# First ten attention units in another order, nine routing constants on GpSimd, second routing tables thirteen steps later

## The chip, the core and the metric

The kernel runs on one core of one Trainium2 chip. The metric is the device time of one execution in microseconds (us). A core has five engines that run their own instruction streams in order: TensorE (PE, matmuls and transposes through the array), VectorE (DVE), ScalarE (ACT), GpSimd (POOL) and SyncE (SP, which here issues most DMAs). An instruction waits at the head of its stream until the semaphores that it names have been raised; what stands behind it waits too.

## The reference

The program is an attention followed by a mixture of experts, with one expert for each token:

```python
q_n, k_n = rmsnorm(q, g_q), rmsnorm(k, g_k)      # 8 batches, 12 heads, 448 tokens, 64 wide
scores = scale * np.matmul(q_n, k_n.transpose(0, 1, 3, 2))
scores = scores - np.max(scores, axis=-1, keepdims=True)
attn = np.exp(scores)
attn = attn / (np.sum(attn, axis=-1, keepdims=True) + 1e-09)
x = np.matmul(attn, v)                           # as 3584 tokens x 768
...
logits = x @ w_gate + modality_bias[modality_id]
e_idx = np.argmax(logits, axis=1)                # one of 8 experts
...
h = np.maximum(x[mask] @ w1[e], 0.0)             # 768 -> 1024
out[mask] = gate_w[mask, None] * (h @ w2[e])     # 1024 -> 768
```

## The kernel before

The attention is cut into 48 units, one for each pair of heads of a batch, and each unit into seven slots; step n = 7u + j is slot j of unit u. The program runs a loop over n from -22 on, and two tables of numbers written out in the source decide at which n each piece of work is issued (PLAN) and, for the second part, at which of its steps (MOE). Since every engine runs its stream in order, these tables are the schedule.

For a unit, q and k are loaded (`ld`, SP's queue), squared and summed (`sq`), turned into reciprocal roots (`rs`), scaled (`norm`, tile xrw), transposed on PE (`tr`, L807: tk for k, tq for q) and copied out of PSUM as a high part and a rounded remainder (tile xw; `parts`, `va`, `vs` choose engine and step). ACT rounds them into w1w, and DMAs on SP's queue move them (the rows w1w<-xw and w2ha<-xw). `sa` is a matmul of the high parts; DVE reduces it to row maxima (at_hlw<-sa). `mt` (L905) transposes the seven maxima, ACT copies them (xw<-mt) and a DMA puts them beside q as an extra row, so that `st` (L921) gives scores less their maximum. ACT exponentiates st from PSUM (r2w<-st, at_w2lw<-st), GpSimd and DVE add up the sums, and `av` (L965) multiplies with v. Lists in PLAN say for which q or k the sum of squares is made on GpSimd (`ps`, a tree of six additions), on ACT (`pa`, eight activations that each accumulate a row) or on DVE; `nv` lists scalings on DVE; `warm` counts matmuls on constants (L1149) that are put between the others on PE.

The seven `sa` of a unit stand ahead of its own `st` slots: `first` gives the step of the first one and `sastep` the distance to the next. In the kernel before, the `mt` of unit 2 is issued at step 5 and its last `sa` at step 6.

Routing constants are made by `tables_consts`, 25 small DVE instructions from index tiles that GpSimd writes at the start. The program puts them on a list (`slow`) at the end of unit 0, and a few are taken from it at every slot.

The second part runs in slots of 256 tokens of one expert, 24 steps each: 8 steps of mm1 (`ph`, L555, x times w1) and 16 of mm2 (`py`, L586). w1 comes as f32 (r) and is split into a rounded part (ACT, CAST w1w<-r) and a remainder (DVE, w1w<-r,w1w), one pair for each quarter of two of the six row blocks; w2 likewise (w2lw<-r2w). `xtr` and `xcp` transpose the tokens and split them (xrw, xw). After mm1, ACT writes the relu hhw and DVE its remainder hlw from PSUM. Which tokens and experts the later slots take is computed by `tables2`, some 60 small DVE instructions (tb_..., L56). From the step under the key 'tab2' on they are on a list from which `little` pops a fixed number at each step; `flush` is the step at which what is left is issued at once. `get` starts the reading of a slot's lists and `fin` finishes them.

Of the kernel before, what the change touches and what calls it, by code (L numbers as in the profile page):

```python
# [1602 lines left out]
```

## Time and profile before

| | |
|---|---|
| median of three runs | 1047.12 us (1045.88 to 1047.6) |
| the profiled execution | 1046.28 us, of which the span is 1044.6 us |
| PE busy | 1002.7 us, 96% of the span, mean granted clock 0.987 |
| DVE, ACT, POOL busy | 768.8 us (74%), 696.9 us (67%), 706.9 us (68%) |
| PE busy, 0 to 110 us | 94.71 us at a clock of 0.92 |
| PE busy, 110 to 500 us | 381.53 us at 1.00 |
| PE busy, 500 to 700 us | 190.62 us at 0.98 |
| PE busy, 700 us to the end | 335.84 us at 0.99 |

The span runs from the first to the last instruction of the program, and the execution's own time is 1.68 us longer. Busy time is the sum over an engine's instructions without overlaps. The clock is that granted to PE, as a share of 2.4 GHz; 0.50 is 1.2 GHz. PE's idle time and its time at half clock are the two ways in which the span exceeds PE's work.

### The profile page before, as it was taken

The page shows a single profiled execution, that of the slowest core. Times are in us where ns is not written, and L with a number is a line of the kernel's source. Part 1 is how long each engine was busy: PE and PEld are TensorE (multiplying, and loading weights), DVE is VectorE, ACT ScalarE, POOL GpSimd, SP SyncE. Part 2 cuts the span into 40 slices and gives each one's busy share as a digit, 9 for nine tenths or more (in the row PEclk, how much of TensorE's full clock was granted, in tenths as well). Part 3 has the DMA queues.
Part 4 walks back from the last instruction along what each step waited for, and adds up shares of the span by engine and source line. Part 5 has one row for each costly group of instructions (what it writes and reads, how often), then busy time and mean ns, then how long its engine had stood idle before and what let it go on. Part 6 is the DMA issues. An engine that isn't in the chain of part 4 may idle for free.

```text
span 1044.6 us, 19480 instructions
## 1 busy us (share of the span) xinstructions
PE 1002.7 (96%) x6299; PEld 797.9 (76%) x6299; DVE 768.8 (74%) x1499; ACT 696.9 (67%) x1409; POOL 706.9 (68%) x733
## 2 busy tenths in 40 slices
PE   8889999999999999999899899999999999999996
PEld 7656665665666565555449899999999999999996
DVE  6788887888888788887678966676775667666740
ACT  5768998988999898887564554545554555455630
POOL 4677878888888889888866646556554665566221
PEclk8989999999999999999999899999999999999999
DMA  7767787767787777755753111122181221121070
GB/s 184 167 176 195 190 195 181 185 162 199 171 194 181 184 186 165 189 133 130 193 175 81 43 35 54 48 55 63 39 278 51 63 49 35 43 61 55 26 258 34
DMA packets 174741, 133.32 MB, mean 128 GB/s; under 512 B 119084, under 2 KB 168336, under 8 KB 173476
## 3 DMA queue, kind: packets, MB, share of 16 engines
q1 hardware_dynamic: 148900, 90.63, 36.4%
q0 software_dynamic: 23856, 41.28, 12.5%
q8 instruction: 52, 0.85, 0.4%
q14 instruction: 61, 0.50, 0.1%
q10 hardware_dynamic: 1872, 0.06, 0.1%
HBM read 139.06 MB, written 24.18 MB: 156 GB/s over the span
## 4 chain that ended last, share of the span: by engine, by line
PE 80%; DVE 7%; issue 4%; DMA 3%; ACT 3%; POOL 1%; ACTq 0%; SPq 0%; POOLq 0%; DVEq 0%
PE ph L555 21%; PE py L586 18%; PE st L921 15%; PE av L965 12%; PE sa L894 5%; PE tr L807 3%; DMA w1w<-xw 2%; PE pm L980 2%; DVE at_hlw L55 2%; DVE xw L55 1%; DVE xrw L55 1%; ACT w1w L55 1%; DVE w1w L55 1%; PE pm L996 1%; PE sa L885 1%
## 5 line engine op out<-in xcount | busy, mean ns | idle before, releaser
L555 PE MATMUL ph<-xw,w1w 128*128 128x256 f32 x2016 | 248.5, 285 | 6.0 <-DVE w1w L55 3.8
L55 DVE TENSOR_REDUCE at_hlw<-sa 128x1 f32<-128x448 f32 x336 | 204.4, 613 | 66.9 <-PE sa L894 52.8
L555 PEld LDWEIGHTS ph<-xw,w1w 128*128 128x128 f32 x2016 | 246.2, 193 | 7.9 <-DVE w1w L55 4.2
L921 PE MATMUL st<-w1w 128*128 128x448 f32 x480 | 175.0, 413 | 6.8 <-ACT at_w2lw L55 5.8
L921 PEld LDWEIGHTS st<-w1w 128*128 128x128 f32 x480 | 83.6, 190 | 98.3 <-ACT xw L55 24.2
L55 POOL DMA_INDIRECT xrw<-x_d,i x112 | 133.6, 1193 | 36.1 <-issue 31.9
L55 DVE TENSOR_TENSOR w1w<-r,w1w 128x512 fp32r<-128x512 f32 (+1 forms) x180 | 108.7, 648 | 32.1 <-ACT w1w L55 32.1
L55 POOL DMA_INDIRECT r2w<-in_moe_w_dram,tb_w2i x48 | 53.3, 1110 | 116.2 <-DVE w2lw L55 110.6
L55 ACT ACTIVATE hhw<-ph 128x512 fp32r<-128x512 f32 x56 | 33.5, 599 | 128.1 <-PE ph L555 128.1
L55 ACT ACTIVATE at_w2lw<-st 128x448 f32<-128x448 f32 x168 | 89.8, 540 | 39.5 <-PE st L921 37.2
L586 PE MATMUL py<-w2lw,hhw 128*128 128x384 f32 x448 | 115.0, 334 | 0.0
L894 PE MATMUL sa<-w1w 128*128 128x448 f32 x282 | 107.4, 382 | 7.5 <-DVE at_hlw L55 6.5
L55 ACT CAST w1w<-xw 64x448 fp32r<-64x448 f32 x188 | 105.6, 561 | 9.8 <-DVE xw L55 6.0
L921 PE MATMUL st<-w1w,w2ha 65*128 65x448 f32 x288 | 101.1, 371 | 2.1 <-DMA w1w<-xw 2.1
L55 ACT CAST w1w<-r 128x512 fp32r<-128x512 f32 (+1 forms) x180 | 102.0, 637 | 0.0
L55 DVE TENSOR_TENSOR w2lw<-r2w,w2ha 128x1536 fp32r<-128x1536 f32 x28 | 49.2, 1758 | 71.2 <-ACT w2ha L55 67.8
L55 ACT ACTIVATE r2w<-st 128x448 f32<-128x448 f32 x168 | 90.0, 540 | 15.2 <-PE st L921 9.5
L55 POOL TENSOR_TENSOR r2w<-r2w 128x448 f32<-128x448 f32 (+1 forms) x69 | 79.2, 1150 | 23.5 <-DVE r2w L55 10.8
L55 POOL TENSOR_TENSOR xrw<-r,at_hlw 112x512 f32<-112x512 f32 x89 | 93.5, 1052 | 1.9 <-POOL w1w L55 0.9
L55 ACT ACTIVATE yw<-py,lt 128x384 f32<-128x384 f32 x55 | 29.0, 577 | 81.3 <-issue 66.6
L586 PEld LDWEIGHTS py<-w2lw,hhw 128*128 128x128 f32 x448 | 81.0, 188 | 0.0
L55 POOL TENSOR_TENSOR r2w<-r2w,at_w2lw 64x448 f32<-64x448 f32 (+1 forms) x46 | 53.1, 1158 | 33.3 <-DVE r2w L55 19.9
(316 smaller groups left out, 2134.3 us busy)
## 6 DMA issues: line engine op xcount, KB each, us to landing
w1w<-xw SPq DMA_DIRECT2D x312, 112.0 KB
r<-in_q_dram SPq DMA_DIRECT2D x48, 224.0 KB
r<-in_k_dram SPq DMA_DIRECT2D x48, 224.0 KB
w2ha<-xw SPq DMA_DIRECT2D x72, 112.0 KB
x_d<-at_w2hb SPq DMA_DIRECT2D x8, 672.0 KB
x_d<-yw SPq DMA_DIRECT2D x8, 672.0 KB
r2w<-in_v_dram SPq DMA_DIRECT2D x24, 128.0 KB
at_w2lw<-in_v_dram SPq DMA_DIRECT2D x24, 128.0 KB
```

Of the source, the lines that this page charges most:

```text
L55: return fn(*a, **kw)
L555: PE.matmul(ps[:, i], lhsT=lt_, rhs=rt_[:, c], start=n == 0, stop=n == 17)
L586: PE.matmul(ps[n][:, :384], lhsT=lt_[:, j, 128 * t : 128 * t + 128], rhs=rt_[:, 384 * n : 384 * n + 384], start=j == 0 and m == 0, stop=j ...
L807: PE.transpose(sp[:, c], src[:, c], idn[:CP, :CP])
L885: PE.matmul(ps[:, :S], lhsT=qm_b[u % 2], rhs=hi_b[u % 2][1], start=True, stop=True)
L894: PE.matmul(ps[:, :S], lhsT=t["qq"][:, h, a : a + 128], rhs=t["kk"][h], start=True, stop=True)
L921: PE.matmul(ps[:, :S], lhsT=l, rhs=t["qq"][:, h] if first else t["ql"][:, h], start=first and (j != 3 or h == 0), stop=not first and (j != ...
L965: PE.matmul(t["av"][o : o + 64, :S], lhsT=vv[r, u_ % 3, j], rhs=t["p"][r, j], start=c == (0, 3)[u_ % 2], stop=c == (3, 2)[u_ % 2])
L980: PE.matmul(R[g][32 * i : 32 * i + 32, :S], lhsT=sel[m], rhs=T[u + i // 2]["cs"][:, i % 2 ^ i // 2], start=m == 0, stop=False, tile_positi ...
L996: PE.matmul(sm[32 * i : 32 * i + 32, :S], lhsT=wg[:, (4 * g + i) % NP], rhs=T[4 * g + i]["xt"], start=False, stop=True, tile_position=(0, ...
```

## The change

Three things change. PLAN has other numbers for the first ten units (steps, engines of single operations, constant matmuls) and for the hand-over to the second part; the `mt` of unit 2 now stands behind all seven of its `sa`. The first nine instructions of `tables_consts` are on GpSimd and are issued behind the first load; the other 16, now `lanes_consts`, stay on DVE and go on the list at the end of unit 5. In MOE, `tables2` begins at step 20 in place of 7 (slot 0's second layer is steps 8 to 23), with 4 instructions for a step in place of 3, and the steps of slots 1 to 5 are written out.

```diff
-PLAN = {'g2': 8, ... 'rushat': 32, ...
...
-('tk', 0): -19, ('tq', 0): -18, ('sa', 0): -15, ... ('mt', 0): -5, ... ('mt', 2): 5, ... ('sa', 2): 0,
-'sastep': {3: 1, 4: 1, 1: 0.5, 2: 1, 0: 1},
-'ps': [(3, 0), (8, 1), (9, 1), (6, 1)], 'pa': [(5, 1), (5, 0), (9, 0), (7, 0)],
...
+PLAN = {'g2': 6, ... 'rushat': 33, ...
...
+('tk', 0): -17, ('tq', 0): -18, ('sa', 0): -14, ... ('mt', 0): -6, ... ('mt', 2): 10, ... ('sa', 2): 2,
+'sastep': {3: 1, 4: 0.7, 1: 0.5, 2: 0.5, 0: 0.7, 6: 1, 5: 1},
+'ps': [(0, 0), (2, 0), (3, 0), (4, 1), (5, 1), (6, 1), (7, 1)],
+'pa': [(2, 0), (3, 1), (4, 1), (5, 1), (6, 1), (7, 0), (9, 0), (9, 1)],
...
-MOE = {'little': 3, ... 'tab2': 7, 'flush': 37, ... ('fin', 3): 42,
+MOE = {'little': 4, ... 'tab2': 20, 'flush': 38, ... ('fin', 3): 37, ... ('xtr', 3, 1): 66, ('xcp', 3, 1): 68,
...
     def tables_consts():
         for tf, ti in iotas:
-            V.tensor_copy(out=tf, in_=ti)
+            GP.tensor_copy(out=tf, in_=ti)
         for w in (0, LW // 2):
-            V.tensor_copy(out=ltb[:, :, :, w].bitcast(I32), in_=i_tok)
-        V.tensor_scalar(out=ie8, in0=i_e[:, 0:NE], scalar1=float(NE), scalar2=None, op0=ALU.add)
+            GP.tensor_copy(out=ltb[:, :, :, w].bitcast(I32), in_=i_tok)
+        GP.tensor_scalar(out=ie8, in0=i_e[:, 0:NE], scalar1=float(NE), scalar2=None, op0=ALU.add)
         for t in (i_ebase, zb[0][:, NCH]):
-            V.tensor_scalar(out=t, in0=i_e[:, 0:NE], scalar1=float(NT), scalar2=None, op0=ALU.mult)
+            GP.tensor_scalar(out=t, in0=i_e[:, 0:NE], scalar1=float(NT), scalar2=None, op0=ALU.mult)
+
+    def lanes_consts():
         V.tensor_scalar(out=pq, in0=ip, scalar1=5, scalar2=None, op0=ALU.arith_shift_right)
...
         load(0)
+        tables_consts()
         load_gains()
...
             if i == 0:
-                slow += deferred(tables_consts) + deferred(gate_consts)
+                slow += deferred(gate_consts)
+            if i == 5:
+                slow += deferred(lanes_consts)
```

At the start of the program, GpSimd's stream had, between the index tiles (IOTA) and the first step of unit 0's reciprocal roots (at_hlw), nothing. Now it reads:

```order
L55 IOTA i_tok 112x32
L55 CAST i_e<-i_e_i 128x16
L55 CAST i_s<-i_s_i 128x18
L55 CAST i_p<-i_p_i 128x1
L55 CAST i_w_105<-i_w_i 128x4
L55 COPY ltb<-i_tok 112x32 x2
L55 TENSOR_SCALAR ie_116<-i_e 128x8
L55 TENSOR_SCALAR i_ebase<-i_e 128x8
L55 TENSOR_SCALAR zb_119<-i_e 128x8
L55 TENSOR_TENSOR xrw<-xrw 112x8x32
```

The nine constants have moved in ahead of the first tree of additions, which sums the squares of unit 0's q and was on DVE as one reduction.

While unit 1's scores run, DVE's stream in the kernel before holds the maxima of unit 3 (sa_3) with the constants between them:

```order
L55 TENSOR_REDUCE at_hlw<-sa_1_636 128x1
L56 CAST i_p<-i_p_i 128x1
L56 CAST i_w_105<-i_w_i 128x4
L56 COPY ltb<-i_tok 112x32
L55 TENSOR_REDUCE at_hlw<-sa_2_655 128x1
L56 COPY ltb<-i_tok 112x32
L55 SCALAR_TENSOR_TENSOR xw<-tr_1_600,gs,xw 128x448
L56 TENSOR_SCALAR ie_116<-i_e 128x8
L56 TENSOR_SCALAR i_ebase<-i_e 128x8
L56 TENSOR_SCALAR zb_119<-i_e 128x8
L55 TENSOR_REDUCE at_hlw<-sa_3_675 128x1
```

In the changed kernel the maxima of unit 3 (the third of them first) stand there with the remainders of k and q, and none of the constants is left:

```order
L55 SCALAR_TENSOR_TENSOR xw<-tr_1_626,gs,xw 128x448
L55 TENSOR_REDUCE at_hlw<-sa_3_699 128x1
L55 STREAM_TRANSPOSE at_w2hb<-at_hhw 128x14x32
L55 TENSOR_REDUCE at_hlw<-sa_4_712 128x1
L55 TENSOR_TENSOR xw<-tr_0_714,xw 128x448
L55 TENSOR_REDUCE at_hlw<-sa_5_734 128x1
```

At the beginning of slot 1 of the second part, DVE's stream in the kernel before holds the last remainders of w1 (w1w<-r1_2) with the second tables between them:

```order
L55 TENSOR_TENSOR w1w_157<-r1_2_155,w1w_157 128x2x256
L56 TENSOR_REDUCE tb_lm_6727<-tb_le_6726 128x1
L56 TENSOR_SCALAR tb_ep_6725<-tb_ep_6725,tb_lm_6727 128x18
L56 TENSOR_TENSOR tb_oh_6728<-tb_ep_6725,i_e_96 128x288
L55 TENSOR_TENSOR w1w_157<-r1_2_155,w1w_157 128x2x256
L56 TENSOR_TENSOR tb_t3_6723<-tb_dd_6722,tb_oh_6728 128x288
L56 TENSOR_REDUCE tb_js_6729<-tb_t3_6723 128x18
L56 TENSOR_TENSOR tb_t3_6723<-tb_cnt_6720,tb_oh_6728 128x288
L55 TENSOR_TENSOR w1w_157<-r1_2_155,w1w_157 128x2x256
```

In the changed kernel these remainders follow each other, and the tables begin behind them and run on to the first remainder of the relu (hlw<-ph1_0):

```order
L55 TENSOR_TENSOR w1w_157<-r1_2_155,w1w_157 128x2x256 x4
L56 TENSOR_TENSOR run7_6917<-zb0_119,i_ebase_117 128x8
...
L55 TENSOR_TENSOR w2lw_6658<-r2w_159,w2ha_160 128x1536
L56 TENSOR_REDUCE tb_ci_6923<-nbp16_122 128x16
...
L56 TENSOR_REDUCE tb_lm_6929<-tb_le_6928 128x1
L55 TENSOR_TENSOR w2lw_6658<-r2w_159,w2ha_160 128x1536
L55 SCALAR_TENSOR_TENSOR hlw_6524<-ph1_0_6987,hhw_6523 128x512
```

## Rows read from the trace of the kernel before

**Rows 1.** Busy time by engine (instructions), clock, DMA share and GB/s, in two stretches
```profile
0.00:110.00 110.00, 94.71 (x502) 66.10 (x503) 86.95 (x186) 79.61 (x225) 73.66 (x119) 0.92 0.73 182
...
120.00:130.00 10.00, 9.57 (x55) 6.20 (x48) 7.73 (x14) 9.69 (x24) 7.48 (x11) 1.00 0.80 188
```

**Rows 2.** Timeline of PE in the first units
```profile
28.97 0.28 PE L905 MATMUL mt<-idn,at_hlw 128*7 128x128 f32 x1 [0.45 <-DVE at_hlw L55]
...
37.52 0.45 PE L921 MATMUL st<-w1w 128*128 128x448 f32 x1
...
45.95 0.64 PE L921 MATMUL st<-w1w 128*128 128x448 f32 x2
...
58.31 0.74 PE L894 MATMUL sa<-w1w 128*128 128x448 f32 x1 [2.65 <-DVE at_hlw L55]
...
63.92 0.57 PE L921 MATMUL st<-w1w 128*128 128x448 f32 x1
...
83.75 0.45 PE L921 MATMUL st<-w1w 128*128 128x448 f32 x1
```

**Rows 3.** Timeline of DVE in the first units
```profile
26.05 0.62 DVE L55 TENSOR_TENSOR xw<-tr,xw 128x448 fp32r<-128x448 f32 x1 [3.00 <-DMA w1w<-xw]
...
51.20 0.18 DVE L56 COPY ltb<-i_tok 112x32 int32<-112x32 int32 x1
...
53.08 3.33 DVE L56 COPY ltb<-i_tok 112x32 int32<-112x32 int32 x1
...
79.58 1.10 DVE L56 SCALAR_TENSOR_TENSOR i_w<-p,i_p 128x1 f32<-128x1 f32 x1
```

**Rows 4.** Timeline of GpSimd in the first units
```profile
6.76 0.24 POOL L56 TENSOR_SCALAR at_hlw<-at_hlw 112x16 f32<-112x16 f32 x1 [4.62 <-DVE at_hlw L55]
...
53.01 2.25 POOL L55 TENSOR_TENSOR at_hhw<-r2w 128x448 f32<-128x448 f32 x2
55.22 1.13 POOL L55 TENSOR_TENSOR r2w<-at_w2lw 128x448 f32<-128x448 f32 x1
56.43 1.12 POOL L55 TENSOR_TENSOR r2w<-r2w,at_w2lw 64x448 f32<-64x448 f32 x1
```

**Rows 5.** Busy time by engine and clock in two stretches behind waits
```profile
60.00:65.00 5.00, 4.26 (x15) 3.75 (x16) 4.10 (x8) 3.91 (x11) 2.90 (x7) 0.53 0.94 246
585.00:590.00 5.00, 5.00 (x23) 5.00 (x24) 4.73 (x22) 0.54 (x2) 4.08 (x4) 0.50 0.27 84
```

**Rows 6.** ACT's groups by form, 0 to 110 us: sums of squares by row
```profile
L55 ACT ACTIVATE xrw<-r 112x64 f32<-112x64 f32 x32 | 7.7, 242 | 0.0
```

**Rows 7.** Timeline of PE, slots 1 to 3 of the second part
```profile
578.79 1.83 PE L555 MATMUL ph<-xw,w1w 128*128 128x256 f32 x14
...
585.00 17.85 PE L555 MATMUL ph<-xw,w1w 128*128 128x256 f32 x127 [2.78 <-DVE w1w L55]
602.69 0.52 PE L586 MATMUL py<-w2ha,hhw 128*128 128x384 f32 x2
...
619.33 17.43 PE L555 MATMUL ph<-xw,w1w 128*128 128x256 f32 x144
...
656.35 0.38 PE L555 MATMUL ph<-xw,w1w 128*128 128x256 f32 x1 [1.51 <-ACT xw L55]
657.07 5.18 PE L555 MATMUL ph<-xw,w1w 128*128 128x256 f32 x41 [0.34 <-DVE xw L55]
```

**Rows 8.** Timeline of DVE, slot 1 of the second part
```profile
572.92 0.69 DVE L55 TENSOR_TENSOR w1w<-r,w1w 128x512 fp32r<-128x512 f32 x1
...
584.26 0.69 DVE L55 TENSOR_TENSOR w1w<-r,w1w 128x512 fp32r<-128x512 f32 x1
...
588.11 1.75 DVE L55 TENSOR_TENSOR w2lw<-r2w,w2ha 128x1536 fp32r<-128x1536 f32 x1
...
590.33 0.68 DVE L55 SCALAR_TENSOR_TENSOR hlw<-ph,hhw 128x512 fp32r<-128x512 f32 x1
...
607.23 3.70 DVE L55 TENSOR_TENSOR w1w<-r,w1w 128x512 fp32r<-128x512 f32 x6
```

More of the change, by code (lines that the diff above doesn't have):

```diff
@@ L34 @@
 ET = mybir.EngineType
-PLAN = {'g2': 8, 's1n': 11, 's1r': 1.1, 'mA': (), 'lA': (), 'pj': (2, 3, 6, 5, 2, 3, 4), 'rtj': 5, 'rushat': 32, 'pe': 't', 'ave': (8, 8, 8, 8), 'avo': (15, 15, 15), 'av3': 9, 'ord': (3, 0, 1, 5, 4, 2, 6), 'xt': (10, 17), 'sm': 4, 'la': 4, 'rc': 6, 'csv': (1,), 'csj': (4, 5), 'csd': (1, 0), 'cse': (2, 2), 'sa': 14, 'mt': 6, 'tk': 22, 'tq': 19, 'nq': 29, 'nk': 25, 'sk': 49, 'sq': 50, 'rs': 46, 'ld': 58, 'first': {('sq', 0): -22, ('sk', 0): -22, ('nk', 0): -20, ('nq', 0): -20, ('sq', 1): -21, ('sk', 1): -20, ('sq', 2): -20, ('sk', 2): -18, ('nk', 1): -16, ('nq', 1): -14, ('tk', 0): -19, ('tq', 0): -18, ('sa', 0): -15, ('tk', 1): -15, ('tq', 1): -13, ('sa', 1): -3, ('mt', 0): -5, ('tk', 2): -7, ('tq', 2): -4, ('nq', 2): -8, ('nk', 2): -13, ('nq', 3): -6, ('nk', 3): -5, ('sq', 3): -11, ('sk', 3): -8, ('sq', 4): -10, ('sk', 4): -11, ('sq', 6): -5, ('sk', 6): 3, ('sk', 7): -6, ('sq', 8): 6, ('sk', 8): 5, ('nk', 7): 22, ('nq', 9): 37, ('tq', 3): 0, ('mt', 1): 1, ('nq', 5): 12, ('mt', 8): 48, ('rs', 0): -21, ('rs', 2): -17, ('nq', 8): 35, ('rs', 5): -6, ('mt', 2): 5, ('nq', 7): 19, ('mt', 5): 29, ('sk', 9): 14, ('tk', 9): 41, ('mt', 6): 35, ('nq', 6): 14, ('sa', 5): 20, ('rs', 8): 10, ('mt', 4): 20, ('nk', 4): 1, ('ld', 9): 5, ('tk', 5): 13, ('tk', 3): -1, ('tk', 4): 6, ('tq', 4): 10, ('ld', 1): -22, ('ld', 2): -21, ('ld', 3): -17, ('ld', 4): -19, ('ld', 5): -21, ('tk', 8): 33, ('sa', 3): 7, ('mt', 3): 18, ('tq', 8): 38, ('nk', 9): 38, ('ld', 6): -18, ('nk', 5): 3, ('sa', 2): 0, ('sq', 5): -15, ('tk', 7): 27, ('tq', 7): 31, ('nq', 4): -3, ('sa', 7): 35, ('tk', 6): 20, ('sq', 9): 19, ('nk', 6): 17, ('sa', 6): 28, ('tq', 9): 45, ('nk', 8): 28, ('sk', 5): -12, ('tq', 5): 15, ('ld', 8): -1, ('sq', 7): -2, ('rs', 1): -19, ('ld', 7): -11, ('tq', 6): 23}, 'rs0': {0: 0, 1: 1, 2: 2, 5: 0, 8: 0}, 'sastep': {3: 1, 4: 1, 1: 0.5, 2: 1, 0: 1}, 'start': -22, 'warm': {5: 5, -6: 14, -18: 1, -17: 4, -19: 1, 4: 1, 3: 1, -5: 1, -22: 10, -11: 3, -4: 0, -20: 1}, 'warmn': 1, 'early': 1, 'late0': 1, 'pmp0': 2, 'ramp': 10, 'pmp': (0, 0, 1, 0, 0, 1, 0), 'nv': [(5, 0), (8, 0), (8, 1), (1, 1), (6, 1), (2, 1), (0, 0)], 'pmpa': (0, 0, 1, 1, 0, 1, 1), 'rush': (1, 1, 2), 'ps': [(3, 0), (8, 1), (9, 1), (6, 1)], 'pa': [(5, 1), (5, 0), (9, 0), (7, 0)], 'rtr': 4, 'sml': 5, 'vs': [(7, 1), (1, 0), (0, 1)], 'vr': [(0, 8)], 'va': [(1, 0), (1, 1), (6, 1), (3, 1), (4, 1), (4, 0), (0, 1), (2, 0)], 'ma': [], 'gain': -21, 'lv0': 0, 'lv1': -8, 'lg': -22, 'lz': (8, 11, 14, 19), 'parts': {(0, 1): (1, 5, 8, 2), (0, 0): (1, 2, 5, 4), (1, 1): (0, 3, 11, 5), (2, 1): (0, 2, 5, 0), (3, 0): (1, 4, 2, 5), (1, 0): (0, 9, 5, 5), (5, 0): (0, 7, 2, 8), (4, 1): (0, 4, 5, 6), (8, 1): (1, 2, 3, 3), (7, 0): (1, 2, 3, 1), (5, 1): (0, 7, 2, 1), (6, 1): (0, 2, 4, 1), (7, 1): (0, 1, 2, 0), (3, 1): (0, 4, 2, 1), (8, 0): (0, 1, 3, 2), (2, 0): (0, 2, 2, 4), (4, 0): (0, 1, 0, 0), (6, 0): (0, 0, 2, 2)}, 'w10': (22, 18, 15), 'x0': 27, 'xr': (0, 1, 4), 'xrd': 2, 'pdef': ((0, 1, 2, 0), (0, 1, 3, 0)), 'nvd': (), 'gc': -12, 'kh': (-16, -7, -7, 3), 'zt': -7, 'pg': (5, 3), 'g1': 33, 'f1': 23, 'x1': (325, 326, 327, 328, 329, 330, 331, 332)}
@@ new lines @@
+PLAN = {'g2': 6, 's1n': 11, 's1r': 1.1, 'mA': (), 'lA': (), 'pj': (2, 3, 6, 5, 2, 3, 4), 'rtj': 5, 'rushat': 33, 'pe': 't', 'ave': (8, 8, 8, 8), 'avo': (15, 15, 15), 'av3': 9, 'ord': (3, 0, 1, 5, 4, 2, 6), 'xt': (10, 17), 'sm': 4, 'la': 4, 'rc': 6, 'csv': (1,), 'csj': (4, 5), 'csd': (1, 0), 'cse': (2, 2), 'sa': 14, 'mt': 6, 'tk': 22, 'tq': 19, 'nq': 29, 'nk': 25, 'sk': 49, 'sq': 50, 'rs': 46, 'ld': 58, 'first': {('sq', 0): -22, ('sk', 0): -22, ('nk', 0): -20, ('nq', 0): -20, ('sq', 1): -21, ('sk', 1): -20, ('sq', 2): -20, ('sk', 2): -18, ('nk', 1): -16, ('nq', 1): -14, ('tk', 0): -17, ('tq', 0): -18, ('sa', 0): -14, ('tk', 1): -15, ('tq', 1): -13, ('sa', 1): -3, ('mt', 0): -6, ('tk', 2): -8, ('tq', 2): -4, ('nq', 2): -7, ('nk', 2): -10, ('nq', 3): -7, ('nk', 3): -4, ('sq', 3): -14, ('sk', 3): -12, ('sq', 4): -10, ('sk', 4): -12, ('sq', 6): -5, ('sk', 6): 7, ('sk', 7): -4, ('sq', 8): 6, ('sk', 8): 8, ('nk', 7): 19, ('nq', 9): 36, ('tq', 3): 0, ('mt', 1): 1, ('nq', 5): 12, ('mt', 8): 49, ('nq', 8): 35, ('mt', 2): 10, ('nq', 7): 21, ('mt', 5): 28, ('sk', 9): 14, ('tk', 9): 41, ('mt', 6): 36, ('nq', 6): 16, ('sa', 5): 20, ('mt', 4): 20, ('nk', 4): 0, ('ld', 9): 8, ('tk', 5): 13, ('tk', 3): 3, ('tk', 4): 6, ('tq', 4): 11, ('ld', 1): -22, ('ld', 2): -22, ('ld', 3): -17, ('ld', 4): -18, ('ld', 5): -19, ('tk', 8): 33, ('sa', 3): 7, ('mt', 3): 16, ('tq', 8): 37, ('nk', 9): 39, ('ld', 6): -14, ('nk', 5): 8, ('sa', 2): 2, ('sq', 5): -16, ('tk', 7): 27, ('tq', 7): 31, ('nq', 4): 3, ('sa', 7): 35, ('tk', 6): 20, ('sq', 9): 12, ('nk', 6): 15, ('sa', 6): 28, ('tq', 9): 44, ('nk', 8): 22, ('sk', 5): -11, ('tq', 5): 14, ('ld', 8): -3, ('sq', 7): -1, ('ld', 7): -10, ('tq', 6): 22, ('rs', 0): -21, ('rs', 1): -18, ('rs', 2): -16, ('rs', 8): 11, ('rs', 5): -7}, 'rs0': {0: 0, 1: 1, 2: 2, 8: 0, 5: 0}, 'sastep': {3: 1, 4: 0.7, 1: 0.5, 2: 0.5, 0: 0.7, 6: 1, 5: 1}, 'start': -22, 'warm': {5: 8, -6: 13, -18: 0, -17: 2, -19: 0, 4: 0, 3: 0, -5: 0, -22: 3, -11: 2, -4: 2, -20: 0, -3: 3, 0: 2, 9: 0, -16: 0, 6: 0, -2: 0, -7: 0, 1: 0, 2: 0, 7: 0, -14: 3, -1: 1, 11: 0, -21: 5, 10: 0, -12: 0, -15: 4, -8: 0, -10: 1, -13: 0}, 'warmn': 1, 'early': 1, 'late0': 1, 'pmp0': 2, 'ramp': 10, 'pmp': (0, 0, 1, 0, 0, 1, 0), 'nv': [(0, 0), (1, 1), (2, 0), (5, 0), (6, 0), (7, 1), (8, 0), (9, 0)], 'pmpa': (0, 0, 1, 1, 0, 1, 1), 'rush': (0, 1, 2), 'ps': [(0, 0), (2, 0), (3, 0), (4, 1), (5, 1), (6, 1), (7, 1)], 'pa': [(2, 0), (3, 1), (4, 1), (5, 1), (6, 1), (7, 0), (9, 0), (9, 1)], 'rtr': 4, 'sml': 5, 'vs': [(0, 1), (2, 1), (3, 1), (4, 0), (7, 0), (8, 0), (9, 1)], 'vr': [(0, 8)], 'va': [(0, 1), (1, 0), (1, 1), (2, 1), (3, 0), (3, 1), (4, 1), (5, 0), (5, 1), (7, 0), (7, 1), (9, 0)], 'ma': [], 'gain': -22, 'lv0': -5, 'lv1': -11, 'lg': -22, 'lz': (9, 14, 14, 19), 'parts': {(0, 1): (1, 8, 8, 4), (0, 0): (3, 3, 3, 4), (1, 1): (0, 4, 11, 6), (2, 1): (0, 2, 5, 2), (3, 0): (2, 4, 2, 9), (1, 0): (0, 7, 5, 5), (5, 0): (0, 7, 2, 6), (4, 1): (1, 2, 5, 7), (8, 1): (1, 5, 4, 3), (7, 0): (1, 5, 3, 4), (5, 1): (1, 9, 4, 2), (6, 1): (0, 5, 2, 0), (7, 1): (0, 0, 4, 4), (3, 1): (0, 4, 3, 2), (8, 0): (0, 5, 5, 4), (2, 0): (0, 6, 4, 2), (4, 0): (0, 0, 1, 1), (6, 0): (0, 0, 2, 1), (9, 1): (0, 1, 5, 0), (9, 0): (0, 2, 0, 0)}, 'w10': (22, 18, 15), 'x0': 30, 'xr': (0, 1, 4), 'xrd': 2, 'pdef': ((0, 1, 2, 0), (0, 1, 3, 0)), 'nvd': (), 'gc': -15, 'kh': (-16, -4, -7, 4), 'zt': 4, 'pg': (5, 3), 'g1': 31, 'f1': 21, 'x1': (325, 326, 327, 328, 327, 329, 330, 332)}
```

2 lines of the change are left out of this document (1 added, 1 removed).

## The prediction, written before the changed kernel was run

> **What bounds the kernel now.** I read the busy times by stretch first: in the first 110 us PE works 94.71 us at a mean clock of 0.92 [rows 1], while the table above shows it almost full afterwards. So a change to the order can only win where PE idles or runs at half clock. PE's waits and its timeline name the places. (1) Before the first scores: unit 0's maxima are transposed at 28.97 us and its first st runs at 37.52 us [rows 2]. (2) Between unit 1 and unit 2: the first st of unit 1 runs at 45.95 us, that of unit 2 at 63.92 us, 17.97 us later, whereas the next two units take (83.75 - 63.92) / 2 = 9.92 us each [rows 2]. PE waits 2.65 us for the maxima on DVE there [rows 2] and then runs at 0.53, near the lower of its two levels, 1.2 GHz [rows 5]. (3) Slot 1 of the second part: mm1 lasts from 578.79 to 602.69 us, 23.90 us, where an undisturbed mm1 of the same 144 matmuls takes 17.43 us [rows 7]: waits for DVE's remainders of w1, the longest of 2.78 us [rows 7], and a stretch at 0.50 behind them [rows 5]. That is 6.47 us. (4) Slot 3: 1.51 and 0.34 us for tokens split late [rows 7].
>
> **Constants off DVE.** What holds DVE in place (2) is one instruction: the second copy of i_tok into ltb takes 3.33 us from 53.08 to 56.41 us, where the first took 0.18 us [rows 3]. GpSimd runs additions back to back from 53.01 to about 56.35 us, and starts the next at 56.43 us [rows 4]: the copy ended when GpSimd paused. Behind it in DVE's stream stand the remainder of k and the next maximum, for which PE waits. The copy and eight smaller constants leave this place; what is late next there is set by ACT's exponentials and by DVE's maxima, which take a steady unit's 9.92 us. The excess is 17.97 - 9.92 = 8.05 us, half clock included. Unit 1 is still part of the ramp (its own data arrive late), so I take 6 us; bounds 2 (only the wait of 2.65 us goes, in part) and 8.05.
>
> The Trainium skill, "SBUF — State Buffer", section "Who interferes with whom", states that a copy or a scalar operation of VectorE may use both port pairs, and that it and GpSimd then exclude each other for a whole instruction. The 3.33 us copy agrees with it. By that rule the 16 constants that stay on DVE remain exposed, which is the third rival below.
>
> On GpSimd the nine fall into 4.62 us in which it waits for the first sum of squares, until 6.76 us [rows 4]. No row shows these instructions there; GpSimd's own smallest scalar operation takes 0.24 us [rows 4], so nine cost about 2.2 us and are hidden. If each took 0.5 us the gap would be just filled. Behind them stands the tree for unit 0's q, now six additions in place of a reduction on DVE; without cover these push unit 0's reciprocal roots, and all up to the first st, by up to 2 us. I take nothing, since the gap's end also waits for q's load and squares.
>
> **The first units' order.** DVE waits 3.00 us, until 26.05 us, for a DMA that moves q and k's parts [rows 3]; SP's queue had loads of later units between these moves, and most now stand behind. Three reductions that stand between unit 0's last maxima on DVE move to ACT, to GpSimd or behind them. mt(0) could come by those 3 us earlier, and the first st with it, as in both orders six of unit 1's sa stand before it. The copy of mt on ACT must keep up: ACT gets two groups of eight row sums ahead of it. I take -3 us; bounds 0 (ACT takes the place of DVE) and -5 (the wait and the reductions).
>
> The price is on ACT: `pa` grows from four entries to eight, so 32 more activations of 0.242 us, 7.7 us by the 32 that the first 110 us hold now [rows 6], each with a read of its accumulator; the squares and copies that leave ACT (nine instructions of a full tile) roughly pay for the reads. Up to 7.7 us more over the first ten units, then, where ACT is 79.61 us busy of 110 but 9.69 of 10 in a late stretch [rows 1]. Most fall in the first 40 us. I take +1; bounds 0 and +3. The seven more constant matmuls lie where PE idles, and cost nothing as long as it does. mt(2) moves behind its last maximum; unit 2's st comes some 15 matmuls later, so it should not wait.
>
> **Tables later.** DVE's remainders of w1 run from 572.92 us; the one that PE waits for until 585.00 starts at 584.26 us and ends at 584.95 us [rows 7, 8]. It is the eighth. Back to back they take 3.70 / 6 = 0.62 us each [rows 8]; with the three token operations of the same tile size between them (2 us, an estimate by these rows) the eight need 7 x 0.62 + 0.69 + 2 = 7.0 us and not 12.0; the 24 table instructions between them took the other 5.0 us, 0.21 each. Without the tables it ends about 5 us earlier, near 580 us, and PE reaches it after 17 matmuls at 0.12 to 0.13 us, at 580.9 us. So both waits go, with the half clock: -6.47 us.
>
> The tables don't vanish: their work now stands ahead of hlw, the remainder that frees the PSUM bank which the third of mm1's four parts needs. hlw of part 0 was at 590.33 us, behind a w2 remainder of 1.75 us [rows 8]. Now I count from 580: 20 tables by 0.21 us, two w2 remainders and hlw itself, 4.2 + 3.5 + 0.7, so hlw ends near 588.4 us; PE wants the bank at 578.79 + 17.43 / 2 = 587.5 us. A wait of a little under 1 us there and at the next part: +1; bounds 0 and +3.5, half clock included. Net -5.5.
>
> Slot 3's tokens are split a few steps sooner relative to use: of 1.85 us I take -1.5; bounds 0 and -1.85. The shift of the lists (get, fin), of SP's reads and of `put` and `route` between 500 and 580 us I set at 0, between -1.5 and +1.5.
>
> **The sum**, from the profiled execution's 1046.28 us: -3 - 6 + 1 - 5.5 - 1.5 = -15, so 1031.3 us; that execution lies 0.84 us below the median of the runs, so for the median I write 1032. Best bounds: -5 - 8 - 6.5 - 1.9 - 1.5 = -23, 1024. Worst: 0 - 2 + 3 - 3 - 0 + 1.5 = -0.5, 1046.6.
>
> **Rivals.**
> - *The first units hand their time on* (chance 0.22). ACT and DVE are the limit as soon as PE no longer stalls: DVE is busy 86.95 of 110 us [rows 1], and the row sums fill ACT. For it: ACT's 9.69 of 10. Against it: the steady units run 9.92 us with the same work. Then places 1 and 2 give 2 us together, and the sum is -2 - 5.5 - 1.5 = -9: 1038.
> - *Tables block the PSUM bank* (0.12). If hlw comes 2 us late, PE idles and falls to half clock as before, and slot 1 gives back the 6.47 us: -8.5 with a little lost in slot 2: 1038 to 1039. For it: my count is 0.9 us short already. Against it: behind the wait of 1.51 us in slot 3, 41 matmuls took 5.18 us [rows 7], 0.126 each, full speed; only the waits of over 2.5 us were followed by half clock.
> - *The constants left on DVE are caught* (0.07), the slower end. The 16 of `lanes_consts` now fall in units 6 to 8. Before, one of them took 1.10 us for a single element [rows 3], and a copy 3.33. If six are held for 3.33 us as that copy was, DVE loses 19 us in a stretch where it has none to spare, PE waits and slows, and the time is 1049. It decides from five of sixteen on, where 16 us of DVE's time outweigh the 15 gained. Against it: the first copy took 0.18 us beside the same kind of GpSimd work [rows 3].
> - *No effect* (0.03): the order is not what held PE, and 1046.
>
> **How the numbers follow.** The forecast, 1032 (its own range 1027 to 1036), has 0.56. The range goes to 1025 below and to 1042 above, which takes in the two rivals at 1038, and leaves out the last two and a tenth of the forecast's tails. A measurement of this kernel can tell 0.2%, 2.1 us, from no change. Faster: 0.56 + 0.22 + 0.12, less their tails, 0.87; same 0.06; slower 0.07.
>
> **What would show it.** Right: no DVE copy into ltb after 10 us; the first st near 34 us and that of unit 2 not over 12 us behind that of unit 1; mm1 of slot 1 in 17.4 to 19 us; no wait for tokens in slot 3; the two half-clock stretches gone. Wrong: GpSimd's tree starting later than 5 us, ACT above 9.5 of 10 in 30 to 100 us with st waiting for it, a wait of ph for hlw with the clock at 0.5, or lane constants of over 1 us in units 6 to 8.

## The result, and the profile after

The changed kernel takes 1030.34 us (median of four runs, 1029.63 to 1032.51) against 1047.09 us for the kernel before in the same session: a ratio of 0.9845, 95% interval 0.9827 to 0.9863. The profiled span falls from 1044.6 to 1029.2 us, by 15.4 us, and the mean granted clock rises from 0.987 to 0.997. The prediction was 1032, with the range 1025 to 1042.

Busy time by engine in the changed kernel (length, PE, PE's weight loads, DVE, ACT, POOL, then clock, DMA share, GB/s); the first row answers to [rows 1]:

```profile
0.00:110.00 110.00, 99.08 (x559) 68.88 (x561) 88.38 (x182) 89.86 (x296) 79.42 (x127) 1.00 0.76 190
...
110.00:500.00 390.00, 378.74 (x2091) 230.22 (x2088) 323.43 (x716) 335.96 (x747) 328.99 (x350) 1.00 0.72 174
500.00:700.00 200.00, 199.14 (x1342) 177.33 (x1341) 154.61 (x318) 111.00 (x183) 141.78 (x113) 1.00 0.30 84
```

In the first 110 us PE is busy for 4.4 us more, at full clock, and between 500 and 700 us it idles for 0.86 us only. PE's timeline in the first units, as [rows 2]: the first `mt`, then the first `st` of units 0 to 3.

```profile
27.56 0.27 PE L907 MATMUL mt<-idn,at_hlw 128*7 128x128 f32 x1
...
34.51 0.45 PE L923 MATMUL st<-w1w 128*128 128x448 f32 x1
...
43.77 0.65 PE L923 MATMUL st<-w1w 128*128 128x448 f32 x2
...
54.93 0.47 PE L923 MATMUL st<-w1w 128*128 128x448 f32 x1 [1.24 <-ACT at_w2lw L55]
...
66.14 1.07 PE L923 MATMUL st<-w1w 128*128 128x448 f32 x4
```

The same four `st` stood at 37.52, 45.95, 62.65 and 73.59 us before. So unit 1 lasts 11.16 us instead of 16.70, and what PE waits for there is ACT's exponentials (1.24 us), no longer DVE. (The prediction took the row at 63.92 us [rows 2] for unit 2's first `st`; it is the second slot's, and the first stands at 62.65.)

A wait of PE for DVE's maxima between the first `mt` and the first `st` has nearly gone as well. PE's timeline of the kernel before, where the clock behind the wait is 0.50 from 34 to 36 us:

```profile
33.98 0.74 PE L894 MATMUL sa<-w1w 128*128 128x448 f32 x1 [2.52 <-DVE at_hlw L55]
```

And of the changed kernel, where it is 1.00:

```profile
31.49 0.47 PE L896 MATMUL sa<-w1w 128*128 128x448 f32 x1 [0.35 <-DVE at_hlw L55]
```

Unit 2 is not the same in every execution. The run e9 below is the changed kernel again, and behind the same two waits for ACT (1.24 and some 1.0 us) its clock falls where it stayed full here. Busy times and clock from 57 to 62 us, first of the changed kernel, then of e9 (columns as above):

```profile
57.00:62.00 5.00, 4.51 (x22) 2.38 (x23) 2.31 (x5) 4.95 (x25) 4.83 (x7) 1.00 0.93 234
```

```profile
57.00:62.00 5.00, 5.00 (x17) 2.12 (x18) 1.35 (x3) 4.01 (x22) 4.43 (x5) 0.68 0.92 242
```

Unit 2 lasts 11.21 us here and in e10, 12.73 in e9, and 14.22 in e7 and e8 (clock 0.50 and 0.56 there); all five have the same first ten units. So the ledger below is that of an execution without this stretch.

The wait and the half clock in slot 1 and the waits in slot 3 are gone too. PE, as [rows 7], mm1 of slots 1 to 4:

```profile
572.92 17.76 PE L557 MATMUL ph<-xw,w1w 128*128 128x256 f32 x144
...
607.16 17.43 PE L557 MATMUL ph<-xw,w1w 128*128 128x256 f32 x144
...
641.08 17.43 PE L557 MATMUL ph<-xw,w1w 128*128 128x256 f32 x144
674.99 17.43 PE L557 MATMUL ph<-xw,w1w 128*128 128x256 f32 x144
```

And DVE in slot 1, as [rows 8]: the last three remainders of w1, the first instruction of the tables behind them, and the first `hlw`, which is done at 581.43 us, just before PE has run the 72 matmuls after which it needs the bank.

```profile
571.57 1.90 DVE L55 TENSOR_TENSOR w1w<-r,w1w 128x512 fp32r<-128x512 f32 x3 [0.27 <-ACT w1w L55]
573.38 0.16 DVE L56 TENSOR_TENSOR run<-zb,i_ebase 128x8 f32<-128x8 f32 x1
...
580.75 0.68 DVE L55 SCALAR_TENSOR_TENSOR hlw<-ph,hhw 128x512 fp32r<-128x512 f32 x1
```

How far the changed kernel is ahead at the same piece of work (its start in the trace before, less that after) gives the ledger:

| at | ahead by | gained since |
|---|---|---|
| first st of unit 0 | 3.01 us | 3.01 |
| first st of unit 1 | 2.18 | -0.83 |
| first st of unit 2 | 7.72 | 5.54 |
| mt of unit 10 | 7.13 | -0.59 |
| mt of unit 44 | 7.40 | 0.27 |
| slot 1 of the second part | 5.87 | -1.53 |
| slot 2 | 12.17 | 6.30 |
| slot 4 | 14.54 | 2.37 |
| end | 15.4 | 0.86 |

Most of the loss ahead of slot 1, 1.28 us between the mt of units 44 and 47, has one place. At 488 us two small DVE instructions of the list fin, which take 0.17 us each elsewhere in this trace (at 554 us), last over 1 us, and they end with GpSimd's additions. PE waits 1.74 us behind them, and the clock falls. DVE's timeline there:

```profile
486.79 1.12 DVE L55 SCALAR_TENSOR_TENSOR i<-t,q 128x8 int32<-128x8 int32 x1
487.94 1.05 DVE L55 CUSTOM_DVE_ANT_0 i<-lt,i 128x16 uint16<-128x16 uint16 x1
```

GpSimd's timeline beside it:

```profile
486.75 1.13 POOL L55 TENSOR_TENSOR r2w<-r2w,at_w2lw 128x448 f32<-128x448 f32 x1 [1.78 <-DVE t L55]
487.85 2.22 POOL L55 TENSOR_TENSOR at_w2lw<-r2w,at_w2lw 128x448 f32<-128x448 f32 x2
```

PE's timeline behind it:

```profile
489.07 0.44 PE L896 MATMUL sa<-w1w 128*128 128x448 f32 x1 [1.74 <-DVE i L55]
```

And busy times and clock in the next stretch (columns as above):

```profile
490.00:495.00 5.00, 5.00 (x18) 1.87 (x17) 1.18 (x3) 1.37 (x4) 3.28 (x4) 0.69 0.40 78
```

### The profile page after: what moved, and what is told of

It is laid out like the page before. It is cut to its first block, busy times and chain, and to the rows that moved or that the text cites. A ratio compares the mean times of both kernels' runs of the same rounds, so it can differ in the third digit from the quotient of the medians.

```text
span 1029.2 us, 19530 instructions
## 1 busy us (share of the span) xinstructions
PE 997.4 (97%) x6313; PEld 794.0 (77%) x6313; DVE 767.7 (75%) x1493; ACT 700.5 (68%) x1464; POOL 721.1 (70%) x735
## 4 chain that ended last, share of the span: by engine, by line
PE 87%; ACT 4%; DVE 3%; DMA 2%; issue 2%; SPq 1%; POOL 1%; ACTq 0%; POOLq 0%; DVEq 0%
PE ph L557 24%; PE py L588 23%; PE st L923 15%; PE av L967 12%; PE sa L896 5%; PE tr L809 3%; PE pm L982 2%; DVE at_hlw L55 1%; ACT xrw L55 1%; ACT w1w L55 1%; PE pm L998 1%; ACT at_w2lw L55 1%; PE sa L887 1%; DMA w1w<-xw 1%; PE pm L992 1%
## 5 line engine op out<-in xcount | busy, mean ns | idle before, releaser
L557 PE MATMUL ph<-xw,w1w 128*128 128x256 f32 x2016 | 244.9, 283 | 0.0
L557 PEld LDWEIGHTS ph<-xw,w1w 128*128 128x128 f32 x2016 | 243.6, 192 | 1.0 <-issue 0.7
L55 POOL DMA_INDIRECT xrw<-x_d,i x112 | 140.1, 1251 | 34.9 <-issue 31.4
L55 POOL DMA_INDIRECT r2w<-in_moe_w_dram,tb_w2i x48 | 57.2, 1191 | 106.2 <-DVE w2lw L55 99.8
L896 PE MATMUL sa<-w1w 128*128 128x448 f32 x282 | 105.3, 376 | 4.7 <-DVE at_hlw L55 2.7
```

The lines of the kernel that those rows point to most:

```text
L55: return fn(*a, **kw)
L557: PE.matmul(ps[:, i], lhsT=lt_, rhs=rt_[:, c], start=n == 0, stop=n == 17)
L896: PE.matmul(ps[:, :S], lhsT=t["qq"][:, h, a : a + 128], rhs=t["kk"][h], start=True, stop=True)
```

## The experiments

Theory A, the prediction's: in unit 1 one instruction, the copy into ltb [rows 3], held DVE, and moving the constants away brings the 6 us. Rival B: the order of the ten units brings them. Runs 1 to 4, 5 to 8 and 9 to 12 were on three chips; on the second the kernel before took 1071.08 us (1047.64 and 1047.34 on the others), so ratios to the kernel before on the same chip are compared, and from traces the distances between rows.

**Parts alone.** Into the kernel before go the constants alone, the new PLAN alone, the new MOE alone, or both tables without the constants.

```diff
 e1:  -            V.tensor_copy(out=tf, in_=ti)
      +            GP.tensor_copy(out=tf, in_=ti)
      ...                                    (the nine, issued behind load(0); the 16 behind unit 5)
 e2:  PLAN of the changed kernel
 e3:  MOE of the changed kernel
 e4:  PLAN and MOE of the changed kernel
```

> The kernel before with the constants alone moved (nine on GpSimd at the start, the other 16 on DVE from the end of unit 5); both tables of numbers as before. Theory A (the copy that GpSimd holds up is what makes unit 1 long): no copy into ltb on DVE, the first st of unit 2 about 12 us behind that of unit 1 in place of 17.97, slot 1 as before; about 6 us less, 1041 (1039 to 1043). Theory B (the new order of the first units makes the gain, the copy is hidden by other late work): 17 us between the two, 1045 to 1047.

> The kernel before with the first table of numbers (PLAN) alone; the constants stay on DVE and are taken from the list from the end of unit 0, the second part as before. Theory A: the first st near 34.5 us, 3 us sooner, but the copies run beside GpSimd's additions again, one of them takes over 2 us, and unit 1 keeps most of its excess; with the 2 us that the new order gives back in units 2 to 9, 1044 (1041 to 1047). Theory B: the gain of units 0 to 2 is there without the constants, 1038 to 1040.

> The kernel before with the second table of numbers (MOE) alone. Theory A (tables between the remainders of w1 make PE wait in slot 1): mm1 of slot 1 in under 18.5 us in place of 23.90, no waits for tokens in slots 3 and 4; 9.5 us less, 1037.5 (1036 to 1040). Rival: the new steps only fit the new hand-over (fin, get, put and the loads of the first slots come at other times); a wait stays in slot 1 or comes at a later slot, 1041 or more.

> The changed kernel with all 25 constants back on DVE, taken from the list from the end of unit 0; both new tables of numbers. Theory A: a copy held up in unit 1 and PE behind it, some 5 to 7 us more than the changed kernel, 1036 (1034 to 1038). Theory B: within 1.5 us of the changed kernel, 1030 to 1032.

| run | median | ratio, 95% interval |
|---|---|---|
| e1, constants | 1047.85 us | 1.0000 (0.9989 to 1.0010) |
| e2, PLAN | 1041.59 | 0.9944 (0.9924 to 0.9963) |
| e3, MOE | 1038.81 | 0.9917 (0.9905 to 0.9929) |
| e4, both tables | 1032.18 | 0.9852 (0.9834 to 0.9870) |

e1 brings nothing, so the constants as moved do not make the gain. The tables make the whole of it, 0.56% and 0.83% by themselves, and e4 can't be told from the changed kernel's 0.9845: in the new order the copy lasts 1.17 us, and the constants are worth 0.7 us by the two ratios, whose intervals allow up to some 3. e2's time lies in theory A's range and not in B's, but its trace is B's: unit 1 lasts 12.17 us with the constants still on DVE. In e1's trace the copy is gone and unit 1 is shorter, 12.51 us, as theory A has it; but unit 2 is longer, 14.42 us instead of 10.94. DVE's timeline of e1 there:

```profile
58.34 1.36 DVE L55 SCALAR_TENSOR_TENSOR r2w<-at_w2lw,half 128x448 f32<-128x448 f32 x1
59.62 2.72 DVE L55 TENSOR_TENSOR xrw<-r,at_hlw 112x512 f32<-112x512 f32 x1
```

GpSimd's:

```profile
56.11 0.62 POOL L56 TENSOR_TENSOR ball<-m,bia 112x256 f32<-112x256 f32 x1
...
57.40 0.73 POOL L56 TENSOR_TENSOR ball<-ball,r2w 112x256 f32<-112x256 f32 x1
58.08 1.14 POOL L55 TENSOR_TENSOR r2w<-at_w2lw 128x448 f32<-128x448 f32 x1
59.30 2.50 POOL L55 TENSOR_TENSOR r2w<-r2w,at_w2lw 64x448 f32<-64x448 f32 x2
61.86 0.58 POOL L56 TENSOR_SCALAR at_hlw<-at_hlw 112x48 f32<-112x48 f32 x1
```

PE's:

```profile
62.94 0.47 PE L896 MATMUL sa<-w1w 128*128 128x448 f32 x1 [2.50 <-DVE at_hlw L55]
```

The scaling of k (xrw<-r,at_hlw) takes 0.68 us where nothing disturbs it, and here 2.72: it ends about 0.5 us after GpSimd's two additions, as the copy had ended with them. A later DVE instruction was held in place of the removed one, and PE's wait of 2.65 us [rows 2] came back as 2.50.

But e1 moves more than the constants. Behind them on the list `slow` stand the gate's constants (`gate_consts`), four of whose instructions run on GpSimd. With the constants gone from the list these come 45 us earlier. GpSimd's timeline of the kernel before:

```profile
103.92 1.00 POOL L56 TENSOR_TENSOR ball<-ball,r2w 112x256 f32<-112x256 f32 x1
```

In e1 they lengthen GpSimd's run by 2.18 us, and its next addition (r2w<-at_w2lw) starts at 58.08 us, right behind them, where it started at 55.22 us before [rows 4]. The scaling in e1 meets these late additions; in the kernel before it ran at 61.54 us for 0.69, when GpSimd had waited since 57.55. So whether the copy's removal alone would gain, with the gate's constants where they were, no run tests. The changed kernel has them early too, from 47.29 to 51.48 us.

e3 shows the tables as predicted, with one wait for the bank, of 0.28 us, which the changed kernel doesn't have (PE's timeline of e3, slot 1):

```profile
578.74 8.79 PE L555 MATMUL ph<-xw,w1w 128*128 128x256 f32 x72
587.81 9.28 PE L555 MATMUL ph<-xw,w1w 128*128 128x256 f32 x72 [0.28 <-DVE hlw L55]
```

**GpSimd's run.** Theory C, formed on e1: it is not the constants but GpSimd's run of instructions without a pause that holds whichever two-input or copying DVE instruction stands beside it. In the kernel before two trees (the sums of squares of units 6 and 8) make that run longer. e5 puts them on DVE; e6 also moves the constants.

```diff
-'ps': [(3, 0), (8, 1), (9, 1), (6, 1)],
+'ps': [(3, 0), (9, 1)],
```

> The kernel before with two entries fewer in ps: the sums of squares of unit 6's k and unit 8's k are one reduction on DVE each in place of six additions on GpSimd; constants on DVE as before. Theory C (between unit 1 and unit 2 GpSimd runs without a pause from 44 to 57.5 us, because two such trees stand there, and any DVE instruction that needs what GpSimd holds waits for the run's end, be it a copy of constants or a scaling): the run is shorter by some 5 us and broken, no DVE instruction of over 2 us, PE's wait of 2.65 us and the half clock behind it gone, the first st of unit 2 under 13 us behind that of unit 1; 1042 (1040 to 1044). Theory D (the load on DVE and ACT as a whole, or the order of PE's own matmuls): two more reductions on DVE, no gain, 1046 to 1049.

> The same two entries taken from ps, and the nine constants on GpSimd at the start, 16 on DVE from the end of unit 5. Theory C: GpSimd's run is broken and DVE has nine instructions fewer in it; like the run without trees alone or 1 to 2 us better, 1041 (1039 to 1043). Theory D: 1046 to 1048, as with the constants alone.

Measured: 1068.27 us, ratio 0.9966 (0.9943 to 0.9989), and 1068.78 us, 0.9970 (0.9944 to 0.9996). Both are a little faster than the kernel before, by 0.34% and 0.30% where theory C gave 0.5% and 0.6%; they can't be told from each other, and e6's interval ends just short of no change. The traces part them. From the timelines of PE, with the DVE instruction there that lasted longest over its usual time:

```
                                  unit 1   unit 2   st of unit 0   mt of      DVE instruction held between
                                                    to unit 3      unit 10    50 and 70 us (over its usual time)
before                            16.70    10.94    36.07          135.15     copy, 3.33 (+3.15)
e3 (first units as before)        16.66    12.09    37.92          135.94     copy, 3.28 (+3.10)
e1 constants                      12.51    14.42    35.98          135.86     scaling of k, 2.72 (+2.04)
e5 no trees                       12.46    11.78    33.85          133.75     copy, 1.13 (+0.95)
e6 no trees, constants moved      11.26    10.05    30.75          130.02     none over +0.5
changed                           11.16    11.21    31.63          128.02     none
changed, again (e9)               11.14    12.73    32.90          128.96     none
```

In e5 the copy lasts as long as the one addition beside it, 1.14 us from 53.29, and PE's wait for the maxima behind it is 0.47 us and not 2.65: a shorter run makes a shorter hold. With the constants alone moved PE loses the time again one unit later; with both edits nothing is held, and unit 10 comes 5.1 us earlier than before. From st of unit 0 to unit 3 the order of before differs by 1.9 us between two profiles (before and e3), and that of the changed kernel lies between 31.47 and 35.43 us in five (e7, e8 and e10 with it); so e5's 2.2 us is not clearly outside that, e6's 5.3 us is, in one profile. e5's profile is that of its slowest execution, 1075.10 us. The timed gain of e6, 0.3%, is less than its profile shows, on the chip that was slower for every kernel; that part is open.

**Dates or engines.** Which half of PLAN does it? e11 has the changed kernel with the five lists that choose engines (nv, ps, pa, vs, va) as before; e12 the changed kernel with everything else of PLAN as before. e9 is the changed kernel again. The output of e11 is off by 0.1 relative, and which of its operations brings that is open; so only its waits in the first 110 us count as evidence, with that reserve, and not its time.

```diff
 e11: -lists 'nv', 'pa', 'ps', 'va', 'vs' of the changed kernel
      +those of the kernel before
 e12: -all other entries of the changed kernel's PLAN ('first', 'sastep', 'parts', 'warm', ...)
      +those of the kernel before
```

> The changed kernel itself, unaltered, so that the next three have it on the same chip. Both theories: 0.9845 of the kernel before, by the interval measured first 0.983 to 0.986.

> The changed kernel with the five lists that choose engines in the first ten units (nv, ps, pa, vs, va) as before; dates, steps and numbers of parts stay new. Theory D1 (it is when the work is issued that takes unit 1's stall away): the first st of unit 2 is still at most 13 us behind that of unit 1, and the time within 3 us of the changed kernel's. Theory D2 (it is that DVE's work goes to ACT and GpSimd): that distance is 16 to 18 us again, with a wait for DVE's maxima of over 2 us, and the time is 5 to 7 us above the changed kernel's.

> The changed kernel with all of PLAN as before but for the five lists that choose engines, which are new; constants on GpSimd and the second tables stay as changed. D1 (dates): a distance of 16 to 18 us between the first st of units 1 and 2, and 6 to 9 us above the changed kernel's time. D2 (engines): a distance of at most 13 us, and the time 2 to 4 us above it (the start's 3 us are lost either way).

Measured: e9 1030.72 us, 0.9837 (0.9823 to 0.9852); e11 1039.97, 0.9927 (0.9913 to 0.9941); e12 1037.65, 0.9912 (0.9895 to 0.9929). Neither theory holds. With old lists unit 1 lasts 13.93 us, more than D1's 13 and less than D2's 16, with a wait of 2.42 us as D2 had it; unit 2 lasts 15.64, and unit 10's mt is at 138.34 us, 3.2 us later than before. With old dates unit 1 lasts 10.83 us, as D2 had it, but the time is 6.9 us above e9's, in D1's range: unit 10's mt is at 135.30, as before. Each half alone has the hold again. DVE's timeline of e11:

```profile
61.73 2.71 DVE L55 TENSOR_TENSOR xrw<-r,at_hlw 112x512 f32<-112x512 f32 x1
```

PE's behind it:

```profile
65.03 0.74 PE L896 MATMUL sa<-w1w 128*128 128x448 f32 x1 [2.42 <-DVE at_hlw L55]
```

DVE's timeline of e12:

```profile
63.20 3.72 DVE L55 TENSOR_TENSOR xrw<-r,at_hlw 112x512 f32<-112x512 f32 x1 [0.39 <-POOL at_hlw L56]
```

GpSimd's beside it:

```profile
63.12 2.25 POOL L55 TENSOR_TENSOR at_w2lw<-r2w,at_w2lw 128x448 f32<-128x448 f32 x2
65.33 1.05 POOL L55 TENSOR_TENSOR xrw<-r,at_hlw 112x512 f32<-112x512 f32 x1
66.33 1.59 POOL L55 TENSOR_TENSOR r2w<-r2w 128x448 f32<-128x448 f32 x1
```

The scaling waits over three of GpSimd's instructions, until 66.38, takes its turn, and GpSimd's next addition is held in turn (1.59 us; 1.14 is usual). In the changed kernel the same scaling meets a pause. GpSimd's timeline of the changed kernel:

```profile
52.66 1.14 POOL L55 TENSOR_TENSOR r2w<-r2w,at_w2lw 64x448 f32<-64x448 f32 x1
54.55 1.47 POOL L55 TENSOR_TENSOR r2w<-r2w,at_w2lw 128x448 f32<-128x448 f32 x1 [0.74 <-ACT at_hlw L56]
```

DVE's:

```profile
54.32 0.68 DVE L55 TENSOR_TENSOR xrw<-r,at_hlw 112x512 f32<-112x512 f32 x1
```

So neither half of the table has the gain; the two together place the scaling in GpSimd's pause. In e12 the start is late as well (unit 1's first `st` at 49.17 us): a tree of the new lists, from 34.28 us, stands ahead of a scaling on GpSimd, and PE waits 1.55 us, until 37.90, to transpose what that scaling writes.

**The hold at 488 us.** e7 and e10 are the changed kernel with the list fin one slot earlier.

```diff
-'x0': 30,
+'x0': 31,
```

> The changed kernel with x0 31 in place of 30: the reading of slot 0's list on DVE (three small instructions, two of which took 1.12 and 1.05 us at 486.8 to 489.0 beside GpSimd's additions, and made PE wait 1.74 us and drop to half clock for 3.4 us) stands one attention slot earlier, where GpSimd waited from 484.97 to 486.75 us. If the hold-up is that of the copy: the three take 0.5 us together, no wait of PE there, no half clock at 490 us; 2.2 us less than the changed kernel, 1028 (1027 to 1029). If the wait is for the list itself (a DMA) or for DVE's load: no gain, 1030 to 1031.

> The changed kernel with the list fin one slot earlier (x0 31 in place of 30). Theory of the hold (a DVE instruction that starts beside GpSimd's additions lasts until GpSimd pauses): the two instructions of 1.12 and 1.05 us at 488 us take 0.17 us each again, the wait of 1.74 us and the 3.4 us at half clock go, and the time is 2 us below the changed kernel's, some 0.998 of it. Rival (the wait only moves to the next slot): the same time as the changed kernel, within 1 us.

e7 measured 1047.67 us, 0.9777 (0.9751 to 0.9803), on the second chip, where the changed kernel wasn't timed. So it was run again beside e9: 1030.99 us, 0.9853 (0.9834 to 0.9871). The trace does what the theory says. DVE's timeline of e10:

```profile
485.81 0.17 DVE L55 SCALAR_TENSOR_TENSOR i<-t,q 128x8 int32<-128x8 int32 x1
486.01 0.17 DVE L55 CUSTOM_DVE_ANT_0 i<-lt,i 128x16 uint16<-128x16 uint16 x1
```

Busy times and clock behind it:

```profile
490.00:495.00 5.00, 4.86 (x26) 3.00 (x23) 2.04 (x4) 3.08 (x8) 4.48 (x5) 1.00 0.41 91
```

From unit 44's mt to unit 47's it takes 31.51 us instead of e9's 33.18, and the profiled spans are 1028.0 and 1030.1 us. But the medians of five are 1030.99 and 1030.72 us: the expected 2 us are not shown in the time. e10's runs spread more (1029.83 to 1033.98) than e9's (1029.88 to 1031.94), and its two slowest have a mean granted clock of 0.994 and 0.990 where the profiled one has 0.997. Where their clock fell no trace shows; a stretch like that in unit 2 of e9 would do it.

**The tables' place.** e8 is the changed kernel with the second tables begun at step 7 as before.

```diff
-'tab2': 20,
+'tab2': 7,
```

> The changed kernel with the second tables beginning at step 7 again (still four instructions for a step, all other steps as changed). Theory A (the tables between the remainders of w1): mm1 of slot 1 waits again, though the remainders stand at other steps and the tables are popped faster; 3 to 6 us more, 1034 to 1036. Rival (the new steps of s1, put and route made the gain, the tables' place does not matter): 1030 to 1031.

Measured: 1055.95 us, 0.9857 (0.9828 to 0.9885); e7, which beside `tab2` differs by `x0` only, had 1047.67 on the same chip, 8.3 us less; 3 to 6 were expected. PE in slot 1 of e8:

```profile
583.94 1.98 PE L557 MATMUL ph<-xw,w1w 128*128 128x256 f32 x14
586.51 0.62 PE L557 MATMUL ph<-xw,w1w 128*128 128x256 f32 x3 [0.58 <-DVE w1w L55]
590.60 17.10 PE L557 MATMUL ph<-xw,w1w 128*128 128x256 f32 x127 [3.48 <-DVE w1w L55]
```

The waits for remainders of w1 [rows 7] are back, and mm1 lasts to 607.54 us, 23.60 us in place of 17.60. One number of the table makes these 6.0 us; what makes the other 2.3 is open.

## Why the prediction was right, and where not

The time, 1030.3 us for 1032, is right, and term by term:

- **Start, -3:** measured -3.01 at the first `st`, and half of it as forecast. DVE's wait of 3.00 us for a DMA [rows 3] is 1.42 us now, and mt(0) comes 1.41 us earlier (27.56 for 28.97), not 3. The other 1.60 us came behind mt(0), where the prediction had no term: there the kernel before waited for DVE's maxima and then ran at a clock of 0.50 from 34 to 36 us, and the changed one hardly waits and stays at 1.00. That the two add up to the forecast's 3 is luck. GpSimd's nine constants took 2.1 us (estimate 2.2) and were hidden; the roots behind them come some 0.6 to 1.2 us later, without effect on the first `st`. 0.83 us of the gain is lost in unit 0.
- **Constants off DVE, -6:** the stall shrank by 5.54 us, so the size was right, and the reason failed. The size was partly luck: with the right row for unit 2 (62.65 us) a steady unit takes (83.75 - 62.65) / 2 = 10.55 us and the excess is 16.70 - 10.55 = 6.15 us, not 8.05, so that the 6 us left no room for the ramp. The step that failed is "What holds DVE in place (2) is one instruction". What holds DVE is GpSimd's run (e5, e10, e12); the copy was the instruction that stood there. e1 took it away, shortened unit 1 and gained nothing. The step after it, "what is late next there is set by ACT's exponentials and by DVE's maxima", left out GpSimd's own stream: the gate's constants that come forward into its run, and the next DVE instruction that is then held like the first. The new PLAN shortens unit 1 without the constants (12.17 us in e2). Its lists and dates together took the hold of the scaling away (e11, e12), and in the old order the two trees and the constants together did (e6, by its trace).
- **ACT's price, +1:** 0.59 us between units 2 and 10. ACT's row sums in the first 110 us rose from 32 to 64, 15.3 us; ACT is 89.86 us busy of 110, but PE waits for it about as much as before (2.4 us in the first 110, for 2.1).
- **Slot 1, -5.5:** -6.30. The wait for the bank, which I set at +1, is 0: the last remainder ended some 0.5 us after mm1 began, where I had counted 1.2 us, and PE reached the bank at 572.92 + 17.76 / 2 = 581.8 us, 0.4 us behind `hlw`. e3, with a little less slack, shows how near it was. (The trace has 21 table instructions between the first and the eighth remainder, where the prediction counts 24; the 5.0 us that they took stand.)
- **Slot 3, -1.5:** -2.37, and -0.86 in slot 4. I priced two waits of one slot; mm1 of slot 3 lasted 19.80 us before (653.25 to 673.05), 2.37 more than 17.43, and slot 4 had a wait of 0.34 us of its own that I didn't list.
- **Hand-over, 0 ± 1.5:** +1.26 (0.27 gained, 1.53 lost), from the hold at 488 us. This mechanism had been a rival, for other instructions: of the 16 constants left on DVE (101 to 130 us) one was caught, at 0.96 us, and 15 took 0.13 to 0.39 us each; fin was caught.

So the right sum is in part luck: too large by 0.5 us for the constants, too small by 0.8 in slot 1 and by 1.7 in slots 3 and 4, 0.4 too much for ACT, and against these 1.3 lost in the hand-over and 0.8 in unit 0, which had no term, nearly cancel. The rival "the first units hand their time on" fell: of the 7.72 us at unit 2, 7.13 are left at unit 10. "Tables block the PSUM bank" fell with the wait of 0.

## What to carry to other kernels

When a small DVE instruction lasts as long as GpSimd's neighbours, don't price its removal at its excess: look at what stands behind it in DVE's stream, because that can be held next, and at what the edit brings into GpSimd's run (e1, both), and give that run a pause there or thin it out (e5 and e6 by their traces, the changed kernel). Work that nobody waits for is best put behind the last operand that the matmul engine waits for, and weighed against the next buffer that it delays: here one number moved 6.0 us (e8), with 0.4 us to spare at the buffer. And an edit that gains only together with another, as the two halves of PLAN do here (e11, e12), can't be credited by running the parts one by one.
